# A recurrent-memory attention and gated-feed-forward kernel: the upper half of the spread weights written from partition 0 with a 0/1 scale column, whole strips in six steps at either end, and a new plan

## The chip, the cores and the metric

One Trainium2 chip, one core. The metric is the device time of one execution in microseconds (us). A core has five instruction queues that run beside each other: TensorE (PE, with its weight loads PEld), VectorE (DVE), ScalarE (ACT), GpSimd (POOL) and SyncE (SP, which here only issues DMA transfers). On-chip memory is SBUF (128 partitions) and PSUM (eight banks of 128 x 512 f32).

## The reference, cut to what matters

Two layers with the same weights; each is attention A with a recurrent memory, and then a gated feed-forward B, both on layer-normalized rows and added to their input.

```python
# A: 2048 rows of 512 in 64 segments of 32; H = 32 heads of 128; 8 memory rows
for s in range(64):
    h = concat([mem, x[32*s : 32*s+32]])             # 40 rows
    q, k, v = h @ Wq, h @ Wk, h @ Wv                 # per head
    p = softmax(where(mask, q @ k.T * scale, -1e9))  # 40 x 40 per head
    o = (p @ v per head) @ Wo                        # 40 x 512
    mem = o[:8]; out_s = o[8:]
# B
out = (sigmoid(x @ w_gate) * (x @ w_up)) @ w_down    # F = 1792
# whole: x += A(ln(x)); x += B(ln(x)); the same once more
```

The memory makes the 64 segments of a layer a chain. Everything is bf16 with f32 sums.

## The kernel before, in words

**Steps.** There are 70 steps (`NSTEPS`). In step t the first layer works on segment t and the second on segment t - 6 (`LAG`), side by side: the 40 rows of each stand next to each other as 80 columns of a tile `hT` (dimensions on partitions). In the first six and the last six steps only one layer is at work, with 40 columns. Rows go in blocks of 128 (four segments): layernorm and transposes before a block's steps (`pre1`), and the feed-forward (`ffn`) after them; the second layer's rows come out of the first layer's `ffn`.

**A step** (`emit_step`). The heads go in groups of six (the last of two). For each group: q and k (L834, `bank<-hT,wq_sb/wk_sb`), a copy of both to SBUF on ACT (`qku`), the scores (L848), mask, maximum, exponent, sum and division on DVE and ACT (L862 to L879, tiles `st`, `small`, `pb`), and a transpose of the weights back to PSUM (L891). A transpose takes two heads at once; the weights of head u come out on partitions 0 to 39 and those of head 16 + u on 64 to 103. Two copies, *spreads*, bring them into the tile `ptsb`, which was cleared once at the start: the lower one on partitions 0 to 39 into columns of its own, the upper one on 64 to 103 into others, so that `ptsb` is block-diagonal. Then one matmul gives both heads' product with V (L914, `bank<-ptsb,vsb`, contraction over partitions 0 to 103), ACT copies it (`otsb`), and the output projection adds it up (L932). At the end of a step, eight rows go on as memory (L945) and the rest into `oxT`.

**V.** V is not computed in the step for most rows: 24 of a segment's 32 rows (`XS`) are multiplied with Wv in *passes* of 128 rows (`v_pass`, L682: 32 matmuls of 512 columns), stored in DRAM (`scr`), and fetched into `vsb` (L803). The other 8 rows and the memory's 8 are multiplied in the step itself, in a *strip* (`strips`, L759): 32 matmuls with 32 rows of weights-side data, each into its own 32 partitions of PSUM, and then moved by DMA (L814). In a one-layer step a strip has room for 32 rows of one layer; the steps in `thin` (the first four of the first layer and the last four of the second) use it whole, and fetch only 8 rows from `scr`.

**Start.** Before step 0, eight passes of V for the first layer are listed (`v_group`), with the loads of all weights on SP's queue (`load_weights`). They are mixed into the first steps.

**Order.** Every operation is a task of a planner with engines, durations (`copy_ns`, `mm_ns` and so on), landing times of transfers (`lat`), buffers to take, and keys that it reads and writes. A packed list of priorities (`SEQUENCE`) decides among ready tasks; the planner's forward pass fixes the order of instructions on each engine, and for tasks with two possible engines (copies: ACT or DVE) which one does it. PE's order is thus written down before anything runs. Where the plan leaves PE a gap, `warm` puts *filler* matmuls of zeros (L1150). The copies of `ACT` and `DVE` all stand at lines L1158 and L1160.

Of the kernel before, what the change touches and what calls it, by code (L numbers as in the profile page):

```python
# [14 lines left out]
F32 = mybir.dt.float32  # L15
# [38 lines left out]
;AiJ8T3rAL|Nji^h>nE-)}}C6?#2*O0$8G4ZZdL%K2&sSfSGsr9F5bywiEpw1$9etJ{dj{n8$!UX!b>*%CVi0odWLR>PmMTURN8S`<`QSiresNn(7<<XH_|&hysZ(_+9io+E1yoPuJDs<%HrJ9~e&G  # L54
lO{?#YvSIBvP$R_;9f!1|GAlKk>X8^RhDlpmDnr7kt;6IZnSwn6|>@F3yW-VRO=#$!{s!|Z#sU*>kMf3XXFEnvc7`kKHK|1UA0@05#wb7a7HOlD?Yn#`J@z-(MeZ4Km`1|dy`f+^gMz@=%!FceG>$<
t$84$Kv|p6^^$~XKEw?)j1MY5bdV%#WrWw}B23to{C{XpW!a@PnfSMtcvtJ+x*0jL#Q{bGuEI}JeR4GK!d54vj>OKEncRQml~*<K;u1oaaQ4{bP`bof8*k|Jnvq^F=+Qyw{#`8!eH2|2^ft1nJbm7!
Ab!74vPh6M&l&LAlQ$kp(4RycR@9_lQx%SxC@=;7(#|M{pc-Zvq5^7mctV2pd4al%PqA<vseo$aQ(1$2O&p$$2=)#zF^2|o-u9XqFI-1Mc~jNaoYzdPrv`*zAA!u}T!KRNn7qKAo7WedWKFqAM5iWz
(lO=AI5ErprhTd6f)YVPYmhmHt`^X*krIWOe)K$vkW0fBn6t30v3~xgu9D9|2u?9Qhqxd3g!4-fxZSJdG?KXHi3=~m?P`o5>72)lIpD#^L81>xGR3Ji9|#WNB5L4{0_zR8rRp9-LS`%KDA3>to0^K8
trO%5X$z>-v_0tee?vxx^C`edFc{4p18&9J_1{77`WnlnpP=acza2)_2A~h&p}raH3Y3dS29jhXA=bf9kS8`f0IGrq5@}V)qI^z5??#c29baAb0B$86Cw+{B(m#uPRQTV>59ecM?f~YLiHK_agbl@M
>kXP60ej5O8Z1}7VtH~Tyi}o8Nh6os$k>dRMu$0U)mEux#MGAgPf!AyIq?@8yns1dXj`J(kB*bI#3S~kQG5MPNqKzX18+^sdBXNu6=5{T5Go1Hxs9?O$^vCQ9bSAntpCOL*N`Zy6d6f)8l}XGG}z!f  # L60
@(X9T<!k{a%zpTXjJr(t*vp+7A*WM2OF6JX&M0cCIFbCkn57sI8Q<FmQlDF2|3#N}6qtsBH%lb612z6V*1A9Y_A@HY$+fn$;9u1be-2ErQ~GLxg$2@V7S)+jTIXY3FAmgWqS`b0OT4UpsnQ7R$Uf33
f3q+HJ7f{+pc=}GM~NHQMP)4Ah>|J)wLO*-th<rKO_jdm{nOnoiY#EQdRE4_v%h|2_Nh`rzYRf!MHM6J(w85<_tb^)uriQo7uah{!`vFKpVnQ&1p}V2`ifjs&YA$@K)-I1;sCslWe)kvpEr4NIv$>b
$&(@1<pp8s;j>8S|K3v8wlu5u{sJg=#Rx9i+kw<LbAmj-UaSLL1MiR`VRCa!)$b@Ty6%s&&v4>}u`fQZ;+bdW<Ob3l-pr$_EMZQim=hbKvZ5di1HcO5lfzu>|J(t#K!!VbaFFOoH`q3<{|fuFn_mY>
N#qBHUB~tJpDBZzsN#V-j^HA?Zmp^VMr$l&wigZ!6G+n#Wl6+GCYi0!N}4?hlP<aS#+>w}!5feTN8x0LhVLxzf#j{MokfCkc2tntWi%)%a0+_sm}gKS<%9o?Qc^s3X%0c;+3$S4Zf`X_SMflE&zf_o
wPdTR?W}usM(6@KRBnkbX&xW`@27TFHa+~x-n1p7oNpmCO5t~VLj%|2TqGdh-$%(pp$yz?g00A>HskB6GJ(jKjZ%-2KC^<6@57J>vVrNoqFBsW(8oFdrnld-^_;3!9^BItXakbPlLz4Os~=#Z-UE;R
!5pJ^>pPsd&xhDnEIfA;NtUB2{lc`PNhDMNNNXgUt;Y_V(-IRN%Wwc@PoyIz-ja>r86o>5O#|&@Q_TB8>^5aEi+Hfh*7*WY89q>TGH}y*sZdAq>dlKh{IpyunqlyBE6}`&jeD%QD-bv-@nHELd#&I}
jU>HA@Gs*vv~NJiDWi6~+2-+z=+tAp_2U-kk;Oboz6}CNL=y1tO~SZt|5342>sk+++3Zo%f=GV#H&LgjhVM#tIBp=kP6Cgamu(<{{@8FLGHqAvecHiZs<xJ+H#)9rRR4+)jCexU3mvz-mae3hp`2-3
FEPSk2imif>V(3Sl-{H8mU_cf@*xkxDWOnFwz6c!FJAS;LFerNh?aQ%r4=4mH~gLO<$z5b@w4Q@enjX0N~+4I<4bOV<L&QMs{AL~K^68#PBIoXZyYl}7@JBOHk)VpuZay4Mxx^*F7O_4xh24*esQ8o
nJiw4^WFJh!Er-dsLy>K;Nq6yn&qnrwfILB6Ku+Yf&34Qc{UMk`|s*i&*91|h-!IU*TlOI872}YkcIyQYU32w)fOBYHh7v29KW1*UzoOY?kUUI&AMe8gG+bo(Rr{Qy8UIk&{FyxdC->kW!Idi6@8uR
;Yn>=xdDyJPyu4a9-gP~O4R2`^H@-jJf~NgrO%aCsaKOP2@eiTN7^rw3S>Wbb6m7kSk&+$2QO2>z6~d$B|g&kSQ*G4XuZCIrWn%6z&%`X@*9yt%q!`_ig+H}9RUtnAPLxlIczn_Gc%sk$h*ud5=Ya*  # L70
E#TQTKMYUuH2pWDS@=F{f9&PY_1gn%%>V7%1x0GNPa_w<H&lm72r#6MGH3LrUgY|O8=(u_?Q+wJS~O4cerm_Av#Z2y8Tb17OhXF8uz1Ht3k3MJ85>le-CmjBwlyVeo}tG|u?PusV|K{J<!sV?l76ZC
%ok0t)F8`NxWZia7Lj}pQgjV3bO&b*#gar0CKrt~3BPVv)Vc~=+8iqsz&GOhRv{yU0!If&f}=zT7Rloks0+0n;WS4drhidZ!f6XQyo`#U?bClZ@Dy!MUAD0hDv=3naO5w1GD<qB*(a|By8?O?gmhz<
F@Z7VI3sOOjwuE;n~M-gxqA<{L9H#%Lqka1?kjbvp=89ydelGO$}hiNwB=)#{NB&<8sTHg(yhvI2&bKR*=XH8@YK|96fX!s-3kf{;IAkc1j9?HUju>Zfkr^UXoHZkmz!Gf$;xu&+mVOIQ3|QGf6ZOy
Dkx$DU`6y#LGYZS#XgJbwLkowu$5?eQk=BCGYWt?q&H*)+YLHa53A);_H|Du<6t$5-sGTup)YLO1oot!TJR0iI9DO3+pH(TbIiX#L}71)Bp{_!1n-P%ErTQ}%8pG``{MTE`jUbQuon54^`Hu(RWB0P
klS-rS`0NyyY$W{?=R=8q`dqV<v6u;ntyFPA+C1IVTuOo_hYHhUPTz`VwmKi(o$>7>~qN<&ToL1A9!aNYl6b+ypgKcNis7?LeU*i<N-PVs$MYtrQ#naMkiB<N&4IDJ~%k_!`jlV4O9A8pWo+6e&Etf
RW)umy-K7u?Afx}$|cZH512hsVeog)JK&WS@wY<y&$8Y(JcWg%eEPQB)MOG1zmq$sZ6K|d4XJe#Y+r?TqTI*djB1{`D)$Q7Ytlv1AO%K)vXzD;)b}>7KvA~@O<5zyg?!?9T6}4M|4{wIpjPrZ0?j>M
@gv1n_n9|s;dy^fMo<jXM(as<6BL*Srxp>rm&4@*^xU5+llyIJ{~dMh?E`D~elC54%Zg(E^#ZWDD!G}UBVkMSLh0g;2US!Tn66DSu!z#QEQ(<ZA1OXgzHh0*iMg#xqTW0<=XJCfBOR!gd*6OFo<fU;
*<%9I{zm~grt_(TXqn{hgb+gJ0L0vyTy}|E`^2N*?z=mtf=m4C;o?jl_<O>`tbdW2);*XL1xOS;&Kw6*cT?zv$z1K$&_qbYyq>gHj<GS}a3JfD)am1Oe84}~Po4TP90m@#A1Pm3!l9Rf0G^y|em8w`
0rk?#KOKi?&`|f&+0(At6FZ<t_GS^sd*q&X;1e>>6=jRXedTw_zbHdn2t#5}rCeIP@uX3;-scABupggrqaZ`}9UV=B9u`1xGjJWm02J%L{&f95iMdRkWz#zG=-W#3+&7Z5{`ZF=5KV0LU^Oabhbz)B
Y1lTm(kfI^u7L#XF5lf!g_GcSyXGPAV#J3buSt=VQ<@U&_U9%cx0EAw`qy9H&!zJl_~t%Qx<N=xC0TcH=Hk)j^{fCKF7VZX@S?}jE;&zz7M&xbz!UQiD6&>nXM%}%?Xu}gD=O*!0j_6hg}eNe*&A(+  # L80
hsIHMJA8Nny7zcUzP+D!LOLqUHCcjx<x{<=u}f@G5z(I?xMX{YJo^vLjEbpfnH*5ue&&`};ZM#IRGf3}^2S%<UXk%t#&QS+RH?$mzO^)<lsuhPABB{&@CI^9JV2~K%5KLE!-E!o?f+RK6#Y<;2@Wl0
!6Sz*tlq`48-^^bcv^S(?UufRbe64U01iI$b6csPrOM+Ysq)+z&SH8!E1B^uw}t3&@oJa$<PEAhp4{b`2t7Iq{ZEB{FUSWH6nA9p3;0JI*v^3fa!lOvwQQh@m9zpFfQBJB9OT8y6-ufR^eCGDRXn-j
W479R>{rDHRbOQJp|RTD-hZ>gI1oQc^7TKIDN%oZhPR~q^4!xuAOw0P%3TlI3p!6n+jImwNz00+u;^mh(O{bx8L}{YF)fL1T*XHTkg8@2Rzr<Vw_j1ON%E;WH3`uw*3eJi6G1d;aG6tJZB0EfF6~jW
Wq0N<tEz2$iUs=uZV`b)KBAKy<8xEtF1uQl47v*%!@7>o^8W~Lm51dA{?pv6-wtbc?)KzyY<0?)Uq({iTN$`ni=|vw5>R>_(2-(ws&?+ezL5#PPfmD|%it@}#V6PP^YVkXOFbLrB=Fl?)d&xPQZ{LQ
>HmznolcMn8qQ~kEV*a6?l9kAc|iU&RdBW@8fIdr2#P!*{(lmQ{?4{jr!iWgyXpW`+!ipG354+9gj6q~baBf~P#%92N<yTsRN;Z}qU-83x?K#gz<J@`nw`P6C|WS4qrc1JuZc5{Zq{$iLnm0O6PloB
{a~42^GsmQB^>ulcifoh&TZ;tpH$2cy>~8?3eJKQFtFxojwm-+Q0xNrc_A?0pGJh1Jb!re_Md^Lw(8LUX?bKW1@hHS0!H<F9KjWv?=iaYy{e?^5Q)sc`sOk*A+UM!GvkTsU<Ay&fk(UiM-E$ZL7-<T
WR-!@omdRJu*B3a8UzECk$+L9pZs9(DzQbQeFmgsiI!Cd$LDRLaOcOO!Imsy{CR1CNsw2W_YO*~uqS2x0F|0H$FfdJG`xpEtM4j2nvTJyZ(@|aH3>S{?v=|jRbU9*(tIJOQ!QP?b2!>=sT~ey#M{g|
Ni`HC)Y!?O^bIA%4sJCA<(IQ!o$;0^y+n?U5IrSb+=oiICBtPsXe`_`yMAhS?`*V%*2Q-3fJs5Klr;N|!$~GBMNlnROz(}POr(ois0P4WF1p1~2~Axh@Dlr2zRyHe!G1gT4TP2edUwq+sdxj<hdfp;
6_38TbNQ#9(1w}@PUKnDFqvhC<pXN1Imn#6s{igJZY-hx`vyFgV3%=$K9}&@`hD~UfX0%(Xz?Ru!ez$I){HUr&tU5C7OmTkTaYivEc~G$0~Xi+OW@e~_B~4QHj$e-2|Flg?pYi_?k=1m1P)=ZZoFm#
L1+REWb}1eqF)rqa9rOU##hTLKyWmER4yMNXR4WqomuM`8oM$w7yYlyNI^Wm*IEm!RsKgnX1gI{ky?92()eLB@KBvu6t}YRn{`8cW4FzK>$|JXr$j;+7QOW!e@x<ms5wdDMcHYJEXt1U6oCq>pM_(#  # L90
Q69~+ibL`c!31h7r8WEx`XYvvRenMpSc86gBOu(W(q19v{>Z}K7->?t4-r6TD(Bg>r%cCi=Cn-karKT7J*n@Q9keU@OR$6Bx`4e6I&5%~>h}p)l>B<}Q;*y2P-E-<_E&v??9RY2OlUWIkY8zP`PUnL
SWIce0!u#)?h2qFA4@M~TRit(cEJ6(1%|JePjWiE6d3M?nyGh0Tt_S0&FAb&%mM=C?|%;=kwLwn@V6+L8<y5JfER7=FmwaliagfMxN5Vm2Md#aL9uz&#m6CI8)HdODaRG(FzNd~t3dG3HV8%oMv<-O
SC1^^xJGhM$9%<_klNJ6SoP*>iq#-X2&j$*5-RgxaVz+h_t}HgOob=j{&z#iK;GX&iP~VtO6bEg@rv0&K(Eo9dB65=Pm%=8DVD;epB|M%4sqez@#{TCB(?h2AY{|5UQu_FLfj)hgbP1N1F#SFn>*VK
X455aqMK$LX6e$>p1sR*rg1aKX1MPh)+d%irA4cb30-Nr3HkSfc!gF1{&ocA$u+5RjFi%sVzFVwe?g#&kspwl$>q8P%0%@K1heWrrp?~}Lr&PSbR~2`HV9aaEYw2eC8o!2Zi0m9|1$ZB-k8)>xG!HB
2Xi(}O%u`87t*=&;^|RcIBfOnxAUv!W}4N?_GID9V=Ut#YPv|WrDWoSRk$4P#q>SjPwhRfACRwTxcFY)qi%AIXdun)+WS!gTa|TBFG*a4Z%$kNSnx7kMWbz7D0C0%XaioV#*|r=0=LPr`gkUcP-PQd
U<6GHD%|p=qq<w=8wigQ*@@6xUiX%Xlz9gL2?nr=+jho78djz_1Y*v4J=U@XVEehMNC*}GQS<B678b+MVhj+-U3hg^WaDRN7;xBu1ReY07DZWh)nXj)MReJ#o+SSRkRZw;Sk6U__St1fq6t&rq@84B
)3NwvVJl&5ou@J1Jxiw(h1fsReWqmUo#-0oP+RWC%cAz`rUb<tdk2{{9*ovAJnx<LQz5X*Kk|PqU$|>>K$fnxyLI*=0f<`ZjX+}Jx)d=E6aVLLqm}da+GwozMp(6_XUL%|<zH|5?pAoL+u+CYTQ`I!
^BWx)J~dn>k9!~B^z^@U21VKfuL-pDgGfH-8X)30`ex@Bisbx2VhJ%l23s9O+d}SWmPq|Q^~7lc*Or+SDDZtl=V6|vm?RQD?j6E1YASB72H1zE3;ld{wCuSt?T__nGWF~JEn9^))`)IJ?sUt(5$;t!
# [55 lines left out]
class Task:  # L154
    __slots__ = ("eng", "dur", "lat", "fn", "deps", "succ", "tail", "boost", "ndep", "ready", "start", "idx", "on", "fresh", "acq", "rel", "durs", "tick", "prev", "land", "adj", "banks", "rate", "nb")

    def __init__(self, eng, dur, lat, fn, boost):
# [6 lines left out]
        self.adj = {}  # L164
        self.banks = ()
        self.rate = 0.95
        self.nb = 0


class Buf:  # L170
# [283 lines left out]
class Kern:  # L454
# [120 lines left out]
    def load_weights(self):  # L575
# [10 lines left out]
        for h0, n in ((0, 4), (4, 4), (8, 8), (16, 8), (24, 8)):  # L586
# [4 lines left out]
            for b in xb[:3]:  # L591
                self.load_x(b, *self.boot_x[b])
# [629 lines left out]
```

## Time and profile before

| what | value |
|---|---|
| median of 3 runs (lowest, highest) | 1810.51 us (1808.74, 1812.94) |
| the profiled execution: its time, its span | 1809.62 us, 1807.9 us |
| PE busy | 1781.7 us, 99% |
| ACT busy, DVE busy, POOL busy | 1189.6, 1152.3, 580.5 us |
| granted PE clock | 1.000 |
| DMA | 271.19 MB, mean 150 GB/s; first slice 345 GB/s |

Busy times are of one execution under the profiler. A row of the costliest groups reads: line, engine, operation, tiles out<-in, shapes, count | busy us, mean ns of one | idle us of the engine just before such instructions, with what ended it. In a timeline the first two numbers are start and duration in us. PE's matmuls overlap each other, so their durations don't add up to its busy time.

### The profile page before, as it was taken

The numbers are of one execution on the slowest core, as the hardware profiler recorded it, in microseconds if no ns is written. First come the engines' busy times: TensorE is split into PE (matmuls) and PEld (weight loads), VectorE is DVE, ScalarE is ACT, GpSimd is POOL, SyncE is SP. The second block draws the span as 40 slices with busy tenths as digits, with TensorE's granted clock in tenths as the row PEclk, the third lists the DMA queues.
The fourth block names the chain that finished last, engine by engine and source line by source line (L and its number), as shares of the span: only waits on it lengthen the run. The fifth ranks groups of instructions, "written<-read, shape, count | busy, mean of one in ns | idle before, by whom it ended". The sixth has DMA issues, their size and how long they took to land.

```text
span 1807.9 us, 92108 instructions
## 1 busy us (share of the span) xinstructions
PE 1781.7 (99%) x40039; PEld 1524.2 (84%) x40039; DVE 1152.3 (64%) x3919; ACT 1189.6 (66%) x2987; POOL 580.5 (32%) x838
## 2 busy tenths in 40 slices
PE   8999999999999999999999999999999999999998
PEld 4588888988888888989898888988888888889886
DVE  4466665665566666665666667666666676566665
ACT  6666766676667666666766666666665666666664
POOL 6413032423233243323324241323334231333422
PEclk9999999999999999999999999999999999999999
DMA  9825254635455454545546463545546453554543
GB/s 345 277 66 151 58 151 117 196 109 156 136 160 153 129 171 143 144 125 160 160 132 194 128 183 89 167 138 162 155 142 180 122 143 114 157 154 133 170 123 109
DMA packets 136872, 271.19 MB, mean 150 GB/s; under 512 B 32650, under 2 KB 69138, under 8 KB 136466
## 3 DMA queue, kind: packets, MB, share of 16 engines
q0 software_dynamic: 56928, 184.07, 34.4%
q1 hardware_dynamic: 79538, 81.22, 15.6%
q8 instruction: 314, 5.14, 1.2%
q14 instruction: 92, 0.75, 0.1%
HBM read 220.93 MB, written 26.21 MB: 137 GB/s over the span
## 4 chain that ended last, share of the span: by engine, by line
PE 89%; DVE 4%; ACT 3%; DMA 1%; issue 1%; SPq 0%; POOL 0%; ACTq 0%; DVEq 0%; POOLq 0%
PE bank L834 31%; PE bank L932 16%; PE bank L1034 11%; PE bank L682 8%; PE bank L759 7%; PE bank L1058 5%; PE bank L914 4%; PE bank L848 4%; PE bank L891 2%; DVE st L862 1%; ACT ptsb L1158 1%; PE bank L651 1%; ACT qku L1158 1%; DVE small L867 1%; DVE small L874 1%
## 5 line engine op out<-in xcount | busy, mean ns | idle before, releaser
L834 PE MATMUL bank<-hT,wk_sb 128*128 128x80 bf16 (+1 forms) x8960 | 622.2, 198 | 0.8 <-issue 0.7
L834 PE MATMUL bank<-hT,wq_sb 128*128 128x80 bf16 (+1 forms) x8960 | 622.2, 198 | 0.1
L1158 ACT CAST qku<-bank 128x480 bf16<-128x480 f32 (+3 forms) x770 | 387.9, 513 | 220.8 <-PE bank L834 141.3
L834 PEld LDWEIGHTS <-wq_sb 128*128 128x128 bf16 x8960 | 455.2, 99 | 35.6 <-issue 22.2
L834 PEld LDWEIGHTS <-wk_sb 128*128 128x128 bf16 x8960 | 450.9, 99 | 0.6 <-issue 0.6
L862 DVE TENSOR_TENSOR st<-bank,cst 40x240 f32<-40x240 f32 (+3 forms) x768 | 278.3, 367 | 234.3 <-PE bank L848 227.0
L932 PE MATMUL bank<-otsb,wo_sb 128*128 128x80 bf16 (+1 forms) x8960 | 363.4, 198 | 5.4 <-ACT otsb L1158 4.4
L932 PEld LDWEIGHTS <-wo_sb 128*128 128x128 bf16 x8960 | 338.0, 99 | 21.3 <-issue 8.1
L1026 POOL DMA_DIRECT2D wg<-in_B_w_gate_dram x217 | 164.4, 758 | 268.1 <-PE bank L1034 107.6
L1027 POOL DMA_DIRECT2D wu<-in_B_w_up_dram x217 | 163.9, 755 | 259.0 <-PE bank L1034 110.6
L1052 POOL DMA_DIRECT2D wd<-in_B_w_down_dram x217 | 153.7, 708 | 251.6 <-PE bank L914 82.3
L1158 ACT CAST otsb<-bank 128x480 bf16<-128x480 f32 (+3 forms) x420 | 198.0, 483 | 54.2 <-PE bank L914 40.3
L1158 ACT COPY ptsb<-bank 40x240 bf16<-40x240 bf16 (+3 forms) x559 | 177.9, 320 | 46.1 <-PE bank L891 36.6
L872 ACT ACTIVATE st<-st 80x240 f32<-80x240 f32 (+3 forms) x420 | 158.5, 381 | 43.5 <-DVE st L869 40.0
L1034 PE MATMUL bank<-xnT,wg 128*128 128x128 bf16 (+2 forms) x1784 | 171.6, 218 | 0.2 <-ACT xnT L1158 0.2
L1034 PE MATMUL bank<-xnT,wu 128*128 128x128 bf16 (+2 forms) x1784 | 171.1, 218 | 0.0
L874 DVE TENSOR_REDUCE small<-st 80x6 f32<-80x240 f32 (+3 forms) x420 | 151.2, 362 | 29.5 <-ACT st L872 27.1
L641 POOL TENSOR_TENSOR small<-small,cst 128x1 f32<-128x1 f32 (+1 forms) x80 | 45.2, 566 | 379.1 <-DVE small L640 360.9
L848 PE MATMUL bank<-qku 128*128 128x80 bf16 (+1 forms) x2240 | 160.6, 198 | 1.8 <-ACT qku L1158 1.5
L869 DVE TENSOR_TENSOR st<-st,small 80x240 f32<-80x240 f32 (+3 forms) x420 | 154.1, 368 | 3.5
L879 DVE TENSOR_TENSOR pb<-st,small 80x240 bf16<-80x240 f32 (+3 forms) x420 | 153.5, 369 | 4.0
L867 DVE TENSOR_REDUCE small<-st 80x6 f32<-80x240 f32 (+3 forms) x420 | 151.7, 362 | 4.6
(95 smaller groups left out, 2327.7 us busy)
## 6 DMA issues: line engine op xcount, KB each, us to landing
wg<-in_B_w_gate_dram POOLq DMA_DIRECT2D x220, 256.0 KB, 4.4
wu<-in_B_w_up_dram POOLq DMA_DIRECT2D x220, 256.0 KB, 4.3
wd<-in_B_w_down_dram POOLq DMA_DIRECT2D x220, 256.0 KB, 4.3
vsb<-scr SPq DMA_DIRECT2D x476, 48.0 KB
vsb<-sst SPq DMA_DIRECT2D x480, 32.0 KB
scr<-vst SPq DMA_DIRECT2D x120, 96.0 KB
wk_sb<-in_A_Wk_dram SPq DMA_DIRECT2D x10, 384.0 KB
wq_sb<-in_A_Wq_dram SPq DMA_DIRECT2D x10, 384.0 KB
```

The costliest lines, as they stand in the source:

```text
L834: nc.tensor.matmul(o_ap, lhsT=W[:, c, h * P:(h + 1) * P], rhs=mv(c), start=(c == 0), stop=(c == DC - 1))
L848: nc.tensor.matmul(s_all(SB)[:, w0 + i, :], lhsT=fview(qku[:, i, 0, 0:1], [(1, P)]), rhs=qku[:, i, 1, 0:ncol], start=True, stop=True)
L862: pl.add("DVE", dve_ns(n, True), lambda gsz=gsz, hs=hs, st=st, SB=SB, pj_=pj_, npj_=npj_, mk=mk, idx=idx: nc.vector.tensor_tensor(out=st[p ...
L867: pl.add("DVE", dve_ns(n), lambda hs=hs, st=st, mx=mx: nc.vector.tensor_reduce(out=mx[pr, hs], in_=st[pr, hs], axis=AX.X, op=ALU.max), r=s ...
L869: pl.add("DVE", dve_ns(n), lambda gsz=gsz, hs=hs, st=st, mx=mx: nc.vector.tensor_tensor(out=st[pr, hs], in0=st[pr, hs], in1=mx[pr, hs].uns ...
L872: pl.add("ACT", act_ns(n), lambda hs=hs, st=st: nc.scalar.activation(out=st[pr, hs], in_=st[pr, hs], func=ACTF.Exp, scale=self.scale), r=s ...
L874: pl.add("DVE", dve_ns(n), lambda hs=hs, st=st, sm=sm: nc.vector.tensor_reduce(out=sm[pr, hs], in_=st[pr, hs], axis=AX.X, op=ALU.add), r=s ...
L932: nc.tensor.matmul(WB[:, c * ncol:(c + 1) * ncol], lhsT=self.wo[:, h, c * P:(c + 1) * P], rhs=otsb[:, hl, 0:ncol], start=(h == 0 and c == ...
L1026: pl.add("POOL", 760, lambda wg=wg, fs=fs: nc.gpsimd.dma_start(out=wg[:], in_=self.wgv[:, :, fs]), r=[("wo", self.H - 1)], w=[gk] + bt, la ...
L1027: pl.add("POOL", 760, lambda wu=wu, fs=fs: nc.gpsimd.dma_start(out=wu[:], in_=self.wuv[:, :, fs]), r=[("wo", self.H - 1)], w=[uk] + bt, la ...
L1034: nc.tensor.matmul(gu[:, 2 * i + k, 0:n], lhsT=W[:, c, i * P:(i + 1) * P], rhs=xnT[:, c, rw], start=(c == 0), stop=(c == DC - 1))
L1158: nc.scalar.copy(out=dst, in_=src)
```

## The change

Five things are changed; lines of the diff that are left out are marked with "...".

1. The upper spread reads and writes partitions 0 to 103 in place of 64 to 103, and multiplies with a column that is 0 on partitions 0 to 63 and 1 above. On ACT that is an activation `Copy` with a scale column, on DVE a `tensor_scalar`. The plan charges ACT 93 ns more for it.
2. `thin` has all six one-layer steps at either end instead of four.
3. So fewer rows need a V pass: in place of the pass of blocks 0 and 1 there is a strip (`v_strip`) for 32 rows and a *half pass* (`v_half`: 2 x 16 matmuls with 64 columns of output partitions) for 64; in place of the pass of block 14 in the second layer, another half pass.
4. The start: blocks 2 and 14 come first, blocks 0 and 1 later; Wv is loaded in eight parts, each from the third on after the part two places before it has landed.
5. The planner: other landing times, a slower bus at first, own starting times of the engines, and a new `SEQUENCE`.

```diff
 SEQUENCE = ...
-    BUS, LEAD, TAIL, BIG, ROOM, POOL0 = 345.0, 2000.0, 1900.0, 300000, 1.0, 2000.0
+    BUS, BUS0, SLOW, BIG, ROOM, TAIL = 345.0, 290.0, 18000.0, 300000, 1.0, 1200.0
+    LEAD = {"SP": 1000.0, "POOL": 1800.0}
+    FIRST = {"PE": 0.0, "ACT": 2040.0, "DVE": 980.0, "POOL": 3500.0, "SP": 750.0}
...
+        self.lower = small[:, 58:59]
-        self.lns = [small[:, 10 * i:10 * i + 10] for i in range(3)]
+        self.lns = [small[:, 10 * i:10 * i + 10] for i in range(4)]
...
+        nc.vector.memset(self.lower, 1.0)
+        nc.vector.memset(self.lower[0:64], 0.0)
...
-        for h0, n in ((0, 4), (4, 4), (8, 8), (16, 8), (24, 8)):
+        for h0, n in ((0, 4), (4, 4), (8, 4), (12, 4), (16, 4), (20, 4), (24, 4), (28, 4)):
...
+            if h0 > 4:
+                tk.after = pl.writer[("wv", h0 - 8)]
...
+    def v_half(self, tile, c0, keys, j, b, q8, r16, i16, boot=False):
+        for s in range(2):
...
+                for q in range(2):
+                    for c in range(DC):
+                        for i in range(2):
+                            k = 4 * s + 2 * i + q
+                            nc.tensor.matmul(vb[q][64 * i:64 * i + 64, :], lhsT=tile[:, c, c0:c0 + 64], rhs=self.wv[:, c, k * 512:(k + 1) * 512],
+                                             start=(c == 0), stop=(c == DC - 1), skip_group_check=True)
...
                 def spread(i=i, nu=nu, ptsb=ptsb, PB=PB):
-                    r = slice(64 * i, 64 * i + L)
+                    r = slice(0, 64 * i + L)
                     pt = PB[r, 0:nu * LW // 2].bitcast(BF16).rearrange("p (u j q) -> p u j q", u=nu, j=2)
-                    return (fview(ptsb[r, 0, i, 0:1], [(nj * LW, nu), (LW, nj), (1, L)]), pt[:, :, 0:nj, :])
-                pl.add(("ACT", "DVE"), copy_ns(nu * nj * L, True), spread, r=[PB], w=[("ptsb", pi, i)])
+                    dst = fview(ptsb[r, 0, i, 0:1], [(nj * LW, nu), (LW, nj), (1, L)])
+                    return (dst, pt[:, :, 0:nj, :]) + ((self.lower[r], "scaled") if i else ())
+                d = copy_ns(nu * nj * L, True)
+                d["ACT"] += 93.0 * i
+                pl.add(("ACT", "DVE"), d, spread, r=[PB], w=[("ptsb", pi, i)])
...
+            if b == self.NBLK - 2:
...
+                self.v_half(self.xvl[q], 0, [("xvl", q, 0), ("xvl", q, 1)], 1, b, 2, 0, 0)
                 return
...
-        self.thin = (range(BLK), range(self.NSEG - BLK, self.NSEG))
+        self.thin = (range(self.LAG), range(self.NSEG - self.LAG, self.NSEG))
...
-        self.v_group([0, 1], {0: p0, 1: p1}, [[(0, 96, 0, 8)], [(0, 0, 0, 24)]])
         self.v_group([2, 14], {}, [[(0, 0, 0, 24)], [(0, 96, 0, 8)]])
         self.v_group([3, 4, 5, 7], {}, cuts)
+        self.load_mem0()
+        p0 = self.pre1(0)
+        p1 = self.pre1(1)
...
+        self.v_strip(lambda c: x0[:, c, 0:32], [("xvl", 2, 0)], 0, 0, 0)
...
+        self.v_half(x0, 64, [("xvl", 2, 1)], 0, 1, 0, 8, 2, True)
...
-                if isinstance(got, tuple) and len(got) == 3:
+                if isinstance(got, tuple) and len(got) == 4:
+                    dst, src, by, _ = got
+                    if tk.on == "ACT":
+                        nc.scalar.activation(out=dst, in_=src, func=ACTF.Copy, scale=by)
+                    else:
+                        nc.vector.tensor_scalar(out=dst, in0=src, scalar1=by, scalar2=None, op0=ALU.mult)
+                elif isinstance(got, tuple) and len(got) == 3:
```

The landing times in the plan change so: fetches of `vsb` from `scr` 5.0 to 4.3 us, strips' rows 3.5 to 3.2 us, weights of the feed-forward 5.2 to 4.7 us, each after the issue's own time.

## The prediction

> **What bounds the kernel now.** First the shares of the span, and the slices that show where TensorE (PE) is not full:
>
> ```profile
> PE 1781.7 (99%) x40039; PEld 1524.2 (84%) x40039; DVE 1152.3 (64%) x3919; ACT 1189.6 (66%) x2987; POOL 580.5 (32%) x838
> ...
> PE   8999999999999999999999999999999999999998
> ```
>
> PE is the bound: only work taken off PE, or a wait in front of it, moves the end. The page shows 26.2 us of idle PE (1807.9 - 1781.7). That hides most waiting, since a matmul's modelled end lies some 0.2 us after its start and covers short gaps. So I went through the start times of all matmuls in the trace and summed what each start-to-start exceeds columns/2.4 ns (a 512-column one starts every 216 ns), where that is over 15 ns: **69.6 us**, of which 9.6 in the first 100 us, 50.3 from 100 to 1700 and 9.6 after. In the 50.3 us the matmul that came late is L914 (the weights' product) for 13.2, L932 for 9.9, L759 for 6.6 (about 0.1 us before each strip), L1002 for 6.5, L834 for 6.1, L848 for 4.3. L914 waits for both spreads of its group, L1158/L1160:
>
> ```profile
> L914 PE MATMUL bank<-ptsb,vsb 104*128 104x80 bf16 x2048 | 140.4, 199 | 3.1 <-ACT ptsb L1158 1.3 <-DVE ptsb L1160 1.0
> ```
>
> Then the spreads themselves, on VectorE (DVE), in the timeline (start, duration, both in us):
>
> ```profile
> 963.23 0.40 DVE L862 TENSOR_TENSOR st<-bank,cst 80x240 f32<-80x240 f32 x1
> 963.67 0.29 DVE L1160 COPY ptsb<-bank 40x240 bf16<-40x240 bf16 x1
> 963.99 0.40 DVE L862 TENSOR_TENSOR st<-bank,cst 40x240 f32<-40x240 f32 x1
> 964.31 0.26 DVE L1160 COPY ptsb<-bank 40x240 bf16<-40x240 bf16 x1
> 964.50 0.38 DVE L867 TENSOR_REDUCE small<-st 80x6 f32<-80x240 f32 x1
> 964.91 0.28 DVE L1160 COPY ptsb<-bank 40x240 bf16<-40x240 bf16 x1
> 965.23 0.42 DVE L1041 SCALAR_TENSOR_TENSOR hff<-th,bank 128x256 bf16<-128x256 f32 x1
> ```
>
> By the program's order the first and third spread are upper halves (partitions 64 to 103), the second a lower one (0 to 39). The lower one starts 0.08 us before its forerunner ends (963.99 + 0.40 against 964.31), and its successor 0.07 us before it ends. An upper one starts 0.03 us after its forerunner ends, and its successor 0.03 us after it. So each upper spread costs DVE 0.10 us twice. Over all upper spreads ScalarE (ACT) shows the same: gaps of about +0.01 to +0.02 us on both sides, where lower ones overlap by 0.10: 0.11 us twice. The plan's costs (`copy_ns`) know nothing of it: 420 upper spreads, some 0.2 us each, 84 us of DVE and ACT time that arrives late.
>
> **What the Trainium skill says.**
> - "VectorE: DVE Perf Modes", section "Two Vector instructions with no wait between them": an instruction whose input or output starts in another 32-partition quadrant than the last one in that memory is held until all earlier ones are done. This is the pattern above, before and behind an upper spread; the trace agrees, and shows it on ACT too.
> - "ScalarE: Activation LUTs", section "What ACT_TABLE_LOAD costs": a pointer operand adds about 93 ns to an ACTIVATE. The trace of before has none on ACT; I take this price.
> - "VectorE: DVE Perf Modes", section "The perf-mode tier table": copy and tensor_scalar on PSUM data both reach up to 2x. The trace has the copy (0.26 to 0.29 us for 240 elements), not the scaled form from PSUM.
> - "TensorEngine Tiling (Array Packing)", section "Tiling Modes": 32-column tiles run four at once, 64-column tiles two. The trace shows the four (below), not the two.
>
> **The change part by part.**
> (1) *V work.* A full pass is 32 matmuls of 512 columns at 0.216 = 6.9 us. A strip is 32 narrow ones, four at once:
>
> ```profile
> 22.79 1.91 PE L759 MATMUL bank<-wv_sb,hT 128*32 128x512 bf16 x32
> ```
>
> that is 1.84 us from start to start in the chain of waits. The built program has 64 full-width V matmuls fewer, 32 of 32 columns and 64 of 64 columns more: two passes go (-13.8), one strip comes (+1.84), two half passes come. At two at once, 32 take 16 x 0.216 = 3.46, plus 0.1 for each of two starts as before a strip: 3.66 each, +7.3. Sum **-4.7 us**. All of it is PE's, which has no cover, so it counts. If 64-column tiles don't overlap, each half pass costs 6.9 + 0.2: +6.9 on the sum. The two more whole-strip steps at either end keep one strip each; 16 fetches of 24 rows become 8 rows, and 16 of 16 strip rows become 32, all SP's: PE sees nothing unless they land late, and L914 has no DMA among its releasers now.
>
> (2) *Filler matmuls* (L1150, no result) stand where the plan expects a gap. In units of 512 columns the first stretch grows from 23.5 to 46.75, and the rest shrinks from 59.5 to 45: 14.5 x 0.216 = **-3.1 us** of gaps filled.
>
> (3) *The start.* In before, useful V work begins here:
>
> ```profile
> 5.61 0.45 PE L1150 MATMUL bank<-hot 128*128 128x512 bf16 x2
> 9.00 0.40 PE L651 MATMUL bank<-cst,xn 128*128 128x128 bf16 x4 [2.95 <-DVE xn L642]
> ...
> 11.88 1.04 PE L682 MATMUL bank<-wv_sb,xvf 128*128 128x512 bf16 x4 [0.15 <-ACT xvf L1158]
> ```
>
> Now 38.25 filler units stand ahead of the first transposes. The first seven took 2.8 us from 1.00 (the array starts slow), the rest go at 0.216: 1.0 + 2.8 + 6.75 = 10.6. Then, with 0.23 for each set of transposes, 2, 3.75 and 2.75 units: 10.8, 11.2, 11.5, 12.3, 12.5, 13.1. V work begins at 13.1 instead of 11.9: **+1.2 us**. The data aren't later: POOL's memsets that now stand ahead of the first POOL power (L641's) end near 7.9, normalized rows follow near 9.4. The weights of V come in eight parts, each but the first two waiting for the one two places before; SP's queue stands behind those waits, wq, wk and wo loads with it. I cost it at nothing because the first 45 us already move 345 GB/s and PE holds V passes to fill with; without that cover, up to 4 us. Take 0, range 0 to +4.
>
> (4) *The spread.* An upper one now starts at partition 0, with a scale column that starts at 0 too: no hold on either side. DVE saves 0.2 us on each of 154 upper spreads (in the built program), 31 us. ACT has 266, saves 0.22 and pays 0.093: 34 us. Neither engine is the bound, so only PE's stalls count. They are late arrivals that the plan didn't foresee; the new plan's costs (copy cost on DVE, 93 ns more on ACT) fit what the chip should do. Lower bound: half of L914's 13.2, 7 us. Upper: L914, L932, L848, L834 and half of the others from 100 to 1700, about 25 to 30. If dearer, below nothing (slower rival). I take L914's nearly whole and a few us of those behind it in ACT's and DVE's queues: **-15 us**. Late next are L932 (for otsb on ACT) and L1002 (for oxT).
>
> (5) *Shorter planned landings* (5.2 to 4.7 us after issue for wg, wu, wd; 5.0 to 4.3 and 3.5 to 3.2 for vsb). Weights land 4.3 to 4.4 us after issue by the page, issue time included, inside the new value: 0. A fourth `lns` buffer, the memsets of the column: DVE has 36% idle, 0.
>
> Sum: -4.7 - 3.1 + 1.2 - 15 = -21.6 on the profiled execution's own 1809.6 (span 1807.9 and 1.7 around it): 1788.0. The median of the runs is 1810.5, 0.9 above it: **1789 us**. About 0.2% (3.6 us) is what a measurement of this kernel tells from no change.
>
> **The rivals.**
> - *Stalls only move* (0.13). PE's order is fixed by a new list; the gaps before L914 could reappear before L932 or L1002. For it: those already hold 16 us that the spread explains only indirectly. Against: 84 us of unforeseen delay is the largest misfit I find. Then only (1) to (3) are left: 1810.5 - 6.6 = 1804, from 1800 to 1809.
> - *The halves don't overlap* (0.05): the change doesn't do what it says. 1789 + 7 = 1796.
> - *Slower: the scaled form is dearer than the hold* (0.12). Place: the 420 upper spreads, in front of L914. If a pointer operand holds too, ACT pays 0.093 more on 266 and DVE at one element per cycle 240/0.96 - 240/1.92 = 0.125 us more on 154: 44 us late. L914 is late in 135 of its 420 groups now; at that share 14 us reach PE: 1804 + 14 = 1818. It decides from about 50 ns more per upper spread than copy and hold cost now (50 ns x 420 x 0.32 = 6.7, all of the -6.6). For it: no such form in the trace. Against: its start partition is that of its neighbours.
> - The forecast has 0.70, its own range 1777 to 1799.
>
> **How the numbers follow.** Faster: 0.70 + 0.05 + 0.10 of the first rival = 0.85; same: 0.03 of the first and 0.02 of the last = 0.05; slower: 0.10. The range from 1777 reaches through both middle rivals to 1807 and leaves out the slow one and the tails.
>
> **What would show it.** The timeline after: upper spreads (104 partitions) that start 0.07 us or more before their forerunner ends; about 0.35 us plus 0.09 on ACT. L914's stalls under 5 us. Half passes of 1.8 us for 16 matmuls. First V matmul near 13.1. Wrong: DVE's scaled form over 0.4 us, 64-column matmuls 0.216 apart, or PE's stall sum still near 69 us.

## The result and the profile after

| | before | after |
|---|---|---|
| median of 4 runs each, same chip (lowest, highest) | 1810.24 us (1808.74, 1812.94) | 1785.35 us (1784.02, 1786.91) |
| ratio, 95% interval | | 0.9861 (0.9844 to 0.9878) |
| the profiled execution: time, span | 1809.62, 1807.9 us | 1784.02, 1782.3 us |

The change saves 24.9 us where the prediction had 21.6; 1785.35 lies in its range. Line numbers have moved, most by some 60: the weights' product L914 is L973 now, the output product L932 is L991, strips L759 are L815, full V passes L682 are L693, the plain spreads are L1230 (ACT) and L1232 (DVE), and the upper spreads have lines of their own, L1222 (ACT) and L1224 (DVE).

The shares of the span and the slices, from the page of after:

```profile
PE 1754.4 (98%) x39870; PEld 1518.0 (85%) x40077; DVE 1142.3 (64%) x3944; ACT 1166.1 (65%) x2960; POOL 575.4 (32%) x827
...
PE   9999999999999999999999999999999999999998
```

PE has 39870 matmuls in the records and 40077 weight loads: 207 matmul records are missing from this trace, so its busy time is too low and the fall from 99% to 98% means nothing. For the same reason the prediction's stall sum (start-to-start times of matmuls, less columns/2.4 ns) can't be taken from this trace. I take it below from the kernel of experiment 7, whose records are complete and which differs from after in one doubled half pass. The row of the weights' product is hit less:

```profile
L973 PE MATMUL bank<-ptsb,vsb 104*128 104x80 bf16 x2048 | 139.2, 199 | 1.7 <-ACT ptsb L1230 0.2
```

1.7 us of idle PE ahead of it instead of 3.1, and missing records can only make the 1.7 too large; of the two spreads, which ended 2.3 us of idle time before, 0.2 us is left. In the timeline of DVE (start, duration), a lower spread, an upper one and their neighbours:

```profile
982.43 0.18 DVE L932 RECIPROCAL small<-small 80x6 f32<-80x6 f32 x1
982.62 0.28 DVE L1232 COPY ptsb<-bank 40x240 bf16<-40x240 bf16 x1
982.82 0.33 DVE L1224 TENSOR_SCALAR ptsb<-bank,small 104x240 bf16<-104x240 bf16 x1
983.07 0.39 DVE L935 TENSOR_TENSOR pb<-st,small 80x240 bf16<-80x240 f32 x1
```

The upper one starts at 982.82, 0.08 us before its forerunner ends, and its successor 0.08 us before it ends. Before, both gaps were +0.03. ACT's timeline shows the same:

```profile
935.28 0.46 ACT L1222 ACTIVATE ptsb<-bank,small 104x240 bf16<-104x240 bf16 x1
935.64 0.55 ACT L1230 CAST otsb<-bank 128x480 bf16<-128x480 f32 x1
```

Its successor starts 0.10 us before it ends; over all 266 the medians are -0.10 on both sides. Last, the instances of both spreads by form (duration as least/median/most ns; on ACT the forms are counted on every second instance only):

```profile
L1230 ACT COPY ptsb<-bank x269: 172/340/368, 79.4 to 1764.3; 40x240 bf16<-40x240 bf16 x99, 40x120 bf16<-40x120 bf16 x27, 40x80 bf16<-40x80 bf16 x7, 40x40 bf16<-40x40 bf16 x2
L1222 ACT ACTIVATE ptsb<-bank,small x266: 288/455/487, 79.5 to 1764.1; 104x240 bf16<-104x240 bf16 x94, 104x120 bf16<-104x120 bf16 x26, 104x80 bf16<-104x80 bf16 x9, 104x40 bf16<-104x40 bf16 x4
L1224 DVE TENSOR_SCALAR ptsb<-bank,small x154: 222/326/345, 52.0 to 1761.8; 104x240 bf16<-104x240 bf16 x102, 104x80 bf16<-104x80 bf16 x39, 104x120 bf16<-104x120 bf16 x9, 104x40 bf16<-104x40 bf16 x4
L1232 DVE COPY ptsb<-bank x151: 159/265/276, 52.2 to 1762.0; 40x240 bf16<-40x240 bf16 x103, 40x80 bf16<-40x80 bf16 x34, 40x120 bf16<-40x120 bf16 x8, 40x40 bf16<-40x40 bf16 x6
```

At 240 elements the median upper spread takes 460 ns on ACT and 330 on DVE, the lower one 351 and 266. The upper one is longer, and yet takes less of its engine's time than before, counted from its forerunner's end to its successor's start, since both overlaps are back.

Where in the span it was gained: the end of each step's `oxT` copy in both traces. Step 0 ends at 86.3 us before and 86.4 after; step 15 is 4.4 us earlier, step 39 10.7, step 55 16.1, step 63 21.7, step 69 26.3. That is some 0.3 us in every step, as a cost would show that sits in every group, and a little more where block 14's half pass and the last six steps stand.

### The profile page after: what moved, and what is told of

Read it like the earlier page. It is cut to its first block, busy times and chain, and to the rows that moved or that the text cites. A ratio compares the mean times of both kernels' runs of the same rounds, so it can differ in the third digit from the quotient of the medians.

```text
span 1782.3 us, 91985 instructions
## 1 busy us (share of the span) xinstructions
PE 1754.4 (98%) x39870; PEld 1518.0 (85%) x40077; DVE 1142.3 (64%) x3944; ACT 1166.1 (65%) x2960; POOL 575.4 (32%) x827
## 4 chain that ended last, share of the span: by engine, by line
PE 91%; DVE 5%; ACT 1%; issue 1%; DMA 1%; SPq 0%; POOL 0%; ACTq 0%; DVEq 0%; POOLq 0%
PE bank L890 32%; PE bank L991 16%; PE bank L1093 10%; PE bank L693 8%; PE bank L815 7%; PE bank L973 4%; PE bank L904 4%; PE bank L1117 4%; PE bank L947 2%; DVE st L918 1%; PE bank L1216 1%; PE bank L662 1%; DVE small L930 1%; DVE small L923 1%; DVE st L925 1%
## 5 line engine op out<-in xcount | busy, mean ns | idle before, releaser
L1230 ACT CAST qku<-bank 128x480 bf16<-128x480 f32 (+3 forms) x770 | 388.5, 513 | 219.3 <-PE bank L890 137.9
L918 DVE TENSOR_TENSOR st<-bank,cst 40x240 f32<-40x240 f32 (+3 forms) x768 | 278.3, 368 | 186.0 <-PE bank L904 177.8
L991 PE MATMUL bank<-otsb,wo_sb 128*128 128x80 bf16 (+1 forms) x8960 | 363.6, 198 | 1.8 <-ACT otsb L1230 0.4
L991 PEld LDWEIGHTS <-wo_sb 128*128 128x128 bf16 x8960 | 336.9, 99 | 16.3 <-issue 2.0
L1230 ACT CAST otsb<-bank 128x480 bf16<-128x480 f32 (+3 forms) x420 | 199.8, 483 | 64.0 <-PE bank L973 51.0
L973 PE MATMUL bank<-ptsb,vsb 104*128 104x80 bf16 x2048 | 139.2, 199 | 1.7 <-ACT ptsb L1230 0.2
```

The lines of the kernel that those rows point to most:

```text
L918: pl.add("DVE", dve_ns(n, True), lambda gsz=gsz, hs=hs, st=st, SB=SB, pj_=pj_, npj_=npj_, mk=mk, idx=idx: nc.vector.tensor_tensor(out=st[p ...
L973: nc.tensor.matmul(fview(OB[:, o:o + 1], [(ncol, 2), (1, L)]), lhsT=self.vsb[halves[u // 8]][0:64 + L, j, (u % 8) * P:(u % 8 + 1) * P], rh ...
L991: nc.tensor.matmul(WB[:, c * ncol:(c + 1) * ncol], lhsT=self.wo[:, h, c * P:(c + 1) * P], rhs=otsb[:, hl, 0:ncol], start=(h == 0 and c == ...
L1230: nc.scalar.copy(out=dst, in_=src)
```

## The experiments

My theory: the spread's starting partition costs about 0.2 us in each of 420 instructions on two engines that aren't the bound, and a part of it reaches PE through the weights' product; V work counts in full besides. The rivals: the new list does it, not the spread; the scaled operand costs as much as the hold; the kernel's first steps decide. "Stall sum" is the prediction's measure, from traces with complete records; "PV" is the part of it between 100 and 1700 us where the late matmul is the weights' product, "Wo" the output product.

| kernel | median us | ratio to before (95%) | span us | stall sum | PV | Wo |
|---|---|---|---|---|---|---|
| before | 1810.24 | 1 | 1807.9 | 69.6 | 13.2 | 9.9 |
| after | 1785.35 | 0.9861 (0.9844 to 0.9878) | 1782.3 | (records missing) | | |
| 1 old spread, new plan | 1800.53 | 0.9938 (0.9923 to 0.9952) | 1800.5 | 65.3 | 9.8 | 6.8 |
| 2 new spread, old plan | 1794.85 | 0.9907 (0.9892 to 0.9922) | 1793.2 | 54.6 | 7.1 | 5.3 |
| 3 scaled, from partition 64 | 1820.20 | 1.0044 (1.0027 to 1.0061) | 1820.7 | 86.1 | 22.7 | 10.4 |
| 4 plain, from partition 0 | 1784.74 | 0.9852 (0.9838 to 0.9867) | 1782.7 | 47.2 | 2.7 | 3.6 |
| 5 shorter first filler | 1785.46 | 0.9857 (0.9838 to 0.9876) | 1784.3 | 50.1 | 4.3 | 4.4 |
| 6 no chained Wv loads | 1786.58 | 0.9861 (0.9847 to 0.9876) | 1787.6 | 52.2 | 5.0 | 3.8 |
| 7 a half pass doubled | 1788.82 | 0.9873 (0.9859 to 0.9888) | 1786.1 | 47.4 | 4.6 | 3.6 |
| 8 no later fillers | 1786.38 | 0.9856 (0.9842 to 0.9871) | 1782.5 | 57.1 | 5.2 | 4.3 |

Each ratio is to before on the same chip: 1811.40 us beside experiments 1 to 4, 1812.12 beside 5 to 8. A ratio's interval is about 0.15% either way, 2.7 us, so a difference of 1 or 2 us between two medians says nothing. A stall sum is of a single execution: experiments 4 to 7, whose upper spreads all start at partition 0, have 47.2 to 52.2 us.

**1. After with the old spread.** Everything of the change but the spread.

```diff
-                    r = slice(0, 64 * i + L)
+                    r = slice(64 * i, 64 * i + L)
-                    return (dst, pt[:, :, 0:nj, :]) + ((self.lower[r], "scaled") if i else ())
+                    return (dst, pt[:, :, 0:nj, :])
```

> The changed kernel with its plan, fillers and V work, but the upper spread again a plain copy on partitions 64 to 103. Theory (the hold): 420 upper spreads hold DVE and ACT again, about 0.2 us each on both sides together, and the plan no longer knows of it; the stalls return. Of the 25 us that the change gained, about 6 come from V work and fillers and stay; 1798 to 1805 us expected. Rival (the new plan made the gain, the spread's form does little): 1785 to 1789 us.

1800.53 us: of the 24.9 us, 15.2 are gone by the medians and 13.9 by the ratios. The row of the weights' product, by form:

```profile
L973 PE MATMUL bank<-ptsb,vsb 104*128 104x80 bf16 x2048 | 140.7, 199 | 2.2 <-DVE ptsb L1232 0.7 <-ACT ptsb L1230 0.4 <-DMA vsb<-sst 0.4
```

Spreads on both engines end idle PE again, and the stalls at this product are 9.8 us. So the new list doesn't do the main part.

**2. Before with the new spread.** Only the scaled spread, its column and its branch, on the old list.

```diff
-                    r = slice(64 * i, 64 * i + L)
+                    r = slice(0, 64 * i + L)
...
+                    return (dst, pt[:, :, 0:nj, :]) + ((self.lower[r], "scaled") if i else ())
```

> The kernel before with its own plan and V work; only the upper spread is written over partitions 0 to 103 times the 0/1 column. Theory (the hold): 12 to 18 us less than before, 1792 to 1798 us, with the plan's order unchanged. Rival (the new plan): 1808 to 1812 us, no change. If the two effects add, this gain and that of the new plan with the old spread sum to 25 us.

1794.85 us, 16.6 below the 1811.40 of before, with the order on PE unchanged. The row of the weights' product (L918 here, L914 in before with 3.1 us):

```profile
L918 PE MATMUL bank<-ptsb,vsb 104*128 104x80 bf16 x2048 | 139.3, 199 | 1.5 <-DVE ptsb L1162 0.2
```

The stall sum falls by 15.0. The spread alone is worth 14 to 17 us on either list, and the rest of the change 8 to 11. The two gains, 16.6 here and 10.9 in experiment 1, add up to 27.5 us where 25 were expected; by the ratios it is 1.55% against 1.39%, within the intervals.

**3. After with the scaled form on partitions 64 to 103.** Same instructions and operand as after; the start differs, and with it the number of partitions, 40 instead of 104.

```diff
-                    r = slice(0, 64 * i + L)
+                    r = slice(64 * i, 64 * i + L)
```

> The changed kernel, its upper spread in the scaled form (same values), but on partitions 64 to 103 with the scale column from the same partitions. Theory (the start partition is what costs): the hold is back and the pointer operand's 0.09 us stays on ACT, so no better than the old copy in the new plan: 1798 to 1812 us; gaps of +0.01 to +0.03 us on both sides of an upper spread on DVE. Rival (the scaled form is by itself the quicker one): 1784 to 1788 us.

1820.20 us: 9 us over before and 8 beyond the upper end of what I had expected. In its DVE timeline both gaps are back at the upper spread:

```profile
1003.30 0.23 DVE L1232 COPY ptsb<-bank 40x240 bf16<-40x240 bf16 x1
1003.54 0.35 DVE L1224 TENSOR_SCALAR ptsb<-bank,small 40x240 bf16<-40x240 bf16 x1
1003.92 0.40 DVE L935 TENSOR_TENSOR pb<-st,small 80x240 bf16<-80x240 f32 x1
```

1003.54 against 1003.53, the end of its forerunner, and 1003.92 against 1003.89. ACT's timeline has the same:

```profile
945.76 0.56 ACT L1230 CAST qku<-bank 128x480 bf16<-128x480 f32 x1 [0.41 <-PE bank L890]
946.34 0.46 ACT L1222 ACTIVATE ptsb<-bank,small 40x240 bf16<-40x240 bf16 x1
946.82 0.40 ACT L928 ACTIVATE st<-st 80x240 f32<-80x240 f32 x1
```

The upper spread starts 0.02 us after the cast ends, and the next 0.02 us after it. The waits of PE by what ended them (us in total, times, longest):

```profile
PE bank L973 <- DVE ptsb L1232: 1.1, 4, 0.5
PE bank L973 <- ACT ptsb L1222: 1.1, 6, 0.2
...
PE bank L973 <- ACT ptsb L1230: 0.8, 4, 0.3
```

These three are spreads ahead of the weights' product, whose stalls rise to 22.7 us. The number of partitions is not the cause: the lower spread in after's timeline, also on 40 partitions but from partition 0, overlaps with its neighbours. It is the start partition that the change gets rid of; the scale is what it pays for that.

**4. After without the scale.** All upper spreads are plain copies of partitions 0 to 103.

```diff
-                    return (dst, pt[:, :, 0:nj, :]) + ((self.lower[r], "scaled") if i else ())
+                    return (dst, pt[:, :, 0:nj, :])
```

> The changed kernel, its upper spread a plain copy of partitions 0 to 103 without the column, so that the upper columns also hold the lower head's weights (the output is another one; amount of work and order are the same). It prices the pointer operand: theory, ACT is freed of 0.09 us on 266 spreads, 25 us of ACT time, and since the plan has that time in its order and PE is the bound, little comes of it: 1780 to 1786 us. Rival (the pointer operand's cost passes to PE): 8 us or more less than the changed kernel, under 1778 us.

1784.74 us, not to be told from after. An upper spread of 240 elements takes a median of 356 ns on ACT here and 460 in after, and 270 and 330 on DVE. Over 266 and 154 spreads that is some 28 and 9 us, and nothing of it arrives at the end.

**5. A shorter first filler.** The first stretch of fillers is cut to 32 units, 32 matmuls in place of 39. In the two profiled executions the transposes start at 9.95 instead of 10.81 us and V work at 12.60 instead of 13.46.

```diff
-                        fill[tk.idx] = (on[0], n)
+                        fill[tk.idx] = (on[0], n if fill else min(n, 4 * 32))
```

> The changed kernel with 32 filler matmuls instead of 39 in front of the first transposes, nothing else. Theory (step 3 of the prediction: the fillers, not the data, set when V work begins, and PE is the bound from there): the first transposes start near 9.5 us instead of 10.8, and the end comes up to 1.3 us earlier, 1784 to 1785.5 us. Rival (something else sets the first steps, so that the late start is made good): 1785 to 1787 us, no change.

1785.46 us, which fits both expectations: a gain of up to 1.3 us is less than these runs can tell, so this decides nothing about the end. The transposes came later than the 9.5 us that I expected, and the traces show why. The first fillers of after, of this kernel and of experiment 7, whose program is that of after up to there:

```profile
1.00 9.98 PE L1216 MATMUL bank<-hot 128*128 128x512 bf16 x39 [1.00 <-DVE small L565]
1.00 9.12 PE L1216 MATMUL bank<-hot 128*128 128x512 bf16 x32 [1.00 <-DVE small L565]
1.00 10.88 PE L1216 MATMUL bank<-hot 128*128 128x512 bf16 x39 [1.00 <-DVE small L565]
```

The same 39 fillers take 9.98 us in one execution and 10.88 in another. At first they start about 0.43 us apart and then 0.216, and the first kind numbers 8 in after, 10 here and 12 in experiment 7. Step 0 ends 1.4 us earlier here than in after, and step 1 0.3; in experiment 7 step 0 ends 1.1 us earlier than in after too, with all its fillers.

**6. No chained loads of Wv.**

```diff
-                if tk.after is not None:
+                if False:
```

> The changed kernel without the waits that hold the loads of the eight parts of Wv to two at a time; the order of instructions is the same on every engine. Theory (step 3: hidden): 1783 to 1787 us. Rival (SP's queue stands behind these waits and the first steps come late for it): 2 to 4 us less, 1781 to 1783 us. Other rival (the waits keep transfers from crowding each other): 1 to 4 us more.

1786.58 us, and the ratio is that of after, 0.9861. Its profiled execution was 3.7 us behind after by step 15, with 52.2 us of stalls; the medians show 1.2 us. Nothing here says that the chain costs time.

**7. A half pass doubled.** Each of the 32 matmuls of block 14's half pass runs twice; the start's half pass is left alone.

```diff
-                for q in range(2):
+                for q in (0, 1) if boot else (0, 0, 1, 1):
```

> The changed kernel with the matmuls of the second layer's half pass (block 14) issued twice, the second time over the first with the same values; nothing else changes. Theory (PE is the bound, V work counts in full, 64-column tiles run two at once): 32 more matmuls at 0.108 us, +3.5 us, 1788 to 1790 us. Rival (PE waits enough there to hide it): 0 to +1 us. Rival (no overlap of two tiles): +7 us, 1792 us.

1788.82 us is over after by 3.5 us by the medians, 3.8 by the spans and 2.2 by the ratios, too coarse to tell full from half. The traces tell it. After's two halves of that pass, and below them this kernel's (32 matmuls each):

```profile
1592.80 1.92 PE L730 MATMUL bank<-wv_sb,xvl 128*64 128x512 bf16 x16
1601.37 1.92 PE L730 MATMUL bank<-wv_sb,xvl 128*64 128x512 bf16 x16
```

```profile
1593.58 3.64 PE L730 MATMUL bank<-wv_sb,xvl 128*64 128x512 bf16 x32
1603.88 3.64 PE L730 MATMUL bank<-wv_sb,xvl 128*64 128x512 bf16 x32
```

16 more matmuls of 512 columns add 1.72 us, 0.108 each: two run at once. Step 60, the last before the half pass, ends 0.65 us later than in after; step 62 ends 4.24 later and step 64 4.25. The 3.6 us between are about twice the 1.72, so V work at this place counts in full.

**8. No fillers after the start.**

```diff
-                        fill[tk.idx] = (on[0], n)
+                        if tk.start < 14000.0:
+                            fill[tk.idx] = (on[0], n)
```

> The changed kernel with the fillers of the first 14 us of the plan only; the 45 units of 512 columns that stand later are left out. Theory (they stand in gaps that PE has anyway, while it waits for DVE or ACT): 1783 to 1788 us. Rival (they stand in front of work that is ready sooner than planned): up to 9 us less, 1776 to 1783 us. Other rival (without them PE's clock drops in the waits): over 1790 us.

1786.38 us. 45 units of fillers are gone, 45 x 0.216 = 9.7 us of PE, and the stall sum is 57.1 instead of the 47.2 to 52.2 of experiments 4 to 7. The closest comparison is experiment 4, whose profiled execution has the same span (1782.7 against 1782.5): 9.9 us more of stalls. What the fillers took is empty now, and the end stays where it was.

## Why the prediction was right

Its main step was right in mechanism and in size: upper spreads that start at partition 64 hold two engines beside the bound, and PE pays for a part of it. The V work was right too. That the sum came within 3.3 us is in part luck: the other three terms net -1.9, where the runs leave about 4 to 6 us beyond the spread and the V work, and they are not what they were called.

For the span as a whole, with the stalls of experiment 7 for after's: V work -4.7; fillers from 83 to 91.75 units, +1.9; stalls from 69.6 to 47.4, -22.2. Together -25.0; the spans differ by -25.6.

**(1) V work, -4.7: held.** The half passes measured 1.92 us for 16 matmuls, first start to last end, at 0.108 each (the step priced them at 0.108 plus 0.1 per start), and experiment 7 shows for block 14 that such work has no cover.

**(2) Fillers, -3.1: the number is of another kind than I took it for.** The later ones did shrink by so much, but a filler is exchanged for empty PE time (experiment 8: 9.7 us of fillers away, about as much more of stalls, the same end). Fewer of them are no gain by themselves. What counts is stalls and later fillers together: after the first 100 us, 59.9 + 12.9 before and 39.8 + 9.7 after, 23.3 less.

**(3) The start, +1.2: near in its times, but no term of the sum.** The start in after's timeline:

```profile
10.81 0.39 PE L662 MATMUL bank<-cst,xn 128*128 128x128 bf16 x4
11.04 0.59 PE L1216 MATMUL bank<-hot 128*128 128x512 bf16 x2
...
12.72 0.76 PE L1216 MATMUL bank<-hot 128*128 128x512 bf16 x3
13.46 1.90 PE L693 MATMUL bank<-wv_sb,xvf 128*128 128x512 bf16 x7
```

The transposes begin at 10.81 instead of 10.6 and V work at 13.46 instead of 13.1, 1.6 us later than before. Part of that is chance: the 2.8 us for the first seven fillers were of one execution. And step 0 doesn't follow the start. Experiments 4, 6, 7 and 8, with the same fillers ahead, begin V work between 13.3 and 14.4 us and end step 0 between 85.3 and 87.1, the earliest start with the latest end; experiment 2, on the old list, begins V work 1.2 us later than before and ends step 0 only 0.3 us later.

What lies ahead of the end of step 0 has changed besides. By the matmuls of experiment 7 there are 4.5 us more of fillers and 3.5 us less of V work: a full pass less (-6.8), the half pass (+3.5), the strip (+1.7), and nine full V matmuls that now come later (-1.9). The stalls up to there are 8.5 us before, 6.7 in experiment 7 and 8.6 in experiment 6, so their fall is not clear of the spread of executions. One new wait is in all traces of the new list; in after's:

```profile
PE bank L693 <- ACT wu L1230: 3.0, 1, 3.0
```

That is PE, waiting once for ACT's copy of a V pass out of PSUM, which in turn waits for the buffer `wu` until its earlier content is stored; ACT's timeline of after has it:

```profile
42.44 0.59 ACT L1230 CAST wu<-bank 128x512 bf16<-128x512 f32 x1 [4.00 <-DMA scr<-wu]
```

Whether this wait uses up what an earlier start would give is open; no run took it away. That the chained loads cost nothing, as stated, agrees with experiment 6.

**(4) The spread, -15: held in mechanism and size, not in its make-up.** Experiment 2 has 16.6 us by the medians and 15.0 by the stalls, experiment 1 has 14 to 15 from the other side. The step took the stalls at the weights' product nearly whole, 13.2, and a few us behind them. On the old list only 6.1 of the 15.0 came from there (13.2 to 7.1); the output product gave 4.6 (9.9 to 5.3), the scores (L848) 1.3, and the last 108 us of the span 2.8. That these add up to what was forecast is luck. With the new list the weights' product falls to 4.6 and the output product to 3.6 (experiment 7), so "under 5 us" came true by both together. "Late next" was half right: `oxT` for L1061 (L1002 before) stayed (6.5 to 5.7), the output product did not.

**What was missing from the sum.** With the old spread the new kernel still gained 10.9 us (8.7 to 13.9 by the interval), where the first rival's price for the plan alone had 6.6. Fewer stalls from the new list would explain the difference, and experiment 1 has 65.3 instead of 69.6; but 4.3 us is no more than stall sums of single executions differ by, so this is argued. Step (5), the landings, was not tried by itself.

**The rivals.** Stalls that only move: no, by experiments 1 and 2. Halves that don't overlap: no, 0.108 per matmul. The scaled form dearer than the hold: not in the change, whose form is never held, but in experiment 3 it is, and there the rival's mechanism is right and its rate too low. It priced 44 us more at 0.32, 14 us. (The 0.32 is misread: the 135 are late matmuls, and they lie in about 108 of the 420 groups.) By the medians of gaps and durations, over the spreads that come without a longer wait, an upper spread takes from its forerunner's end to its successor's start about 0.49 us of ACT in experiment 3 and 0.39 in experiment 1, and 0.40 and 0.34 of DVE. Over 266 and 154 of them that is an estimated 37 us more, and the end moved by 19.7, a rate of 0.5. From experiment 1 to after the same measure falls to 0.26 and 0.17, an estimated 62 us less, for 14 to 15: a rate of 0.2. From after to experiment 4 it falls by 37 us more, for nothing. That the plan's list explains this (time above what it planned is late, time below it has nothing to move up) fits the three, but is argued.

**The prices taken over.** In the Trainium skill, "ScalarE: Activation LUTs", section "What ACT_TABLE_LOAD costs", a pointer operand costs an ACTIVATE about 93 ns; here the scaled form takes 0.10 us more than the plain copy (460 against 356 ns for 104x240, after against experiment 4). The skill's "VectorE: DVE Perf Modes", section "The perf-mode tier table", has copy and tensor_scalar from PSUM in one tier, and the trace agrees: the scaled form took 60 ns more (330 against 270 at 240 elements, 258 against 199 at 80), the same at both lengths, so it is a fixed cost and no slower rate. It is half of the 125 ns that the slower rival gave it. The hold that the same page describes in "Two Vector instructions with no wait between them" appears with the start at partition 64 alone, with the scale and without: gaps of 0.01 to 0.03 us on both sides on DVE in experiments 1 and 3, overlaps of 0.07 to 0.08 in after and experiment 4.

## What to carry to other kernels

Look at the gap on both sides of short instructions, not at their durations: a copy that looked cheap (0.28 us) cost DVE 0.20 us around it, and a longer instruction on more partitions took its place with profit because it starts where its neighbours start. A microsecond on an engine beside the bound has no fixed price: here it was worth about 0.5, 0.2 and nothing, in that order, as the spreads got cheaper. Filler matmuls show where a plan has gaps; count them with the stalls, never as a gain.

## What the runs showed of the hardware that I had not expected

A scaled spread from partition 64 is held like a plain one and pays for its scale as well: its gaps are 0.01 to 0.03 us on both sides, on ACT and on DVE, and 0.10 us more on each of 266 and 0.06 on each of 154 cost 19.7 us at the end. Partitions were nearly free: copies of 104 and of 40 partitions by 240 elements take 356 and 352 ns on ACT, 270 and 266 on DVE (experiment 4). And the slow phase of the first matmuls is not the same in every execution: in the eight profiled executions of kernels with the new list, 7 to 12 fillers came about 0.43 us apart before the rest followed at 0.216, and in the seven of them that have all 39 fillers the first transposes moved with it, from 10.70 to 11.71 us.
